# Order of the copies of turned weights, of the odd head's sign and of the value products in the slots of a top-k attention with a routed expert layer

## The chip, the cores and the metric

The kernel runs on one core of one Trainium2 chip. The metric is the device time of one execution in microseconds (us). A time "before" is given as the median of three runs; the profile is that of one further execution.

## What is computed

The reference makes attention over the 32 largest scores of each row, and puts every resulting token through the one expert that its gate chooses. Cut to what matters:

```python
B, H, S, D = 8, 8, 576, 64
scores = q @ k.T / sqrt(D)                      # per batch and head
kth    = the 32nd largest score of each row
attn   = exp(scores - max), zero where scores < kth, divided by its row sum
x      = (attn @ v) as [B*S, H*D]               # 4608 tokens of 512
e      = argmax(x @ w_gate)                     # one of 8 experts per token
out    = softmax weight * sigmoid(x @ w_output_gate)[e] * (relu(x @ w1[e]) @ w2[e])
```

## The kernel before, in words

Queries are taken 128 at a time: 36 tiles of queries (`NTT`), and in each tile four pairs of heads (`NHP`). One pair of heads of one tile is a **step**; there are 144 (`NSTEP`), and the main loop (L939) runs over them with four more to drain. Each pass of the loop is a slot in which the work of several steps stands, each at another stage. Nothing reorders it: every engine runs its instructions in the order in which the loop issues them. For step i:

- `scores` (L282), called two slots ahead: TensorE makes the scores of both heads in PSUM (L293), and ScalarE copies them to SBUF (L301).
- `gmax` and `rank` (L305, L322): VectorE finds the largest scores of eight groups of columns, and from those the first 24 of each row.
- `below` (L346): ScalarE marks, for each of the two heads, the scores below the 24th (a Sign, L355), and GpSimd adds the marks to the scores (L358). `window` (L372) is VectorE's search for the next eight in that, and `choose` (L380) takes the 32nd score out of them.
- `exps` (L366): ScalarE takes the exponential (L370).
- In slot i+1 the scores under the 32nd are cleared: `weigh` (L396) does it on VectorE (L404). In the first 36 steps (i under `LONE`, which is 36) the odd head of the pair goes another way, and I call these the **lone steps**: `veil` (L408) makes a Sign on ScalarE (L411) and a sum on GpSimd (L414), and `unveil` (L417) takes the exponential of that sum on ScalarE (L420) at the slot's end. There is no exponential of that head in `exps` then.
- In slot i+2 `flip` (L423) turns the weights on TensorE, 128x128 at a time, in three parts of four, one and four pieces (L430), and ScalarE copies each part out of PSUM (L438). I call them first, second and third flip. Their PSUM tiles `pst` come from a pool of two buffers in turn: the third flip writes into the buffer of the first, so it waits for the first flip's copy. The second flip's one piece holds the last 64 columns of the even head and the first 64 of the odd one, so in a lone step it waits for `unveil`.
- In slot i+4, for even i, `attend` (L443) multiplies two steps' weights with the values (L462, "the products with values"), and ScalarE copies the result (L464).

Some slots carry **side work** in the PSUM tile of the second flip: for each tile of queries `gates` (L489) and `rows` (L500) in two slots that follow each other, and one product for each group of tiles (L565). ScalarE copies their results behind the second flip's (L486, L496).

The expert layer's work stands in the same slots, from about step 37 on, one piece of a tile of 128 tokens in each slot (`heavy_piece`, L855): L757 for the first matrix, L772 for the second, and L746 for the turning of the tokens (`turn`, L742), which also takes a `pst` buffer. What remains of it runs after the last step.

In a slot, before the change, TensorE has: first flip, expert piece, second flip with side work, third flip, turning of tokens, scores of step i+2, and for even i the products with values. ScalarE has: the two signs of `below`, the odd head's sign (`veil`), the copy of the last products, the copy of the first flip, the exponentials, the expert piece's result, the copies of the second flip and of side work, that of the third, the turned tokens, the copy of the scores, `unveil`.

Of the kernel before, what the change touches and what calls it, by code (L numbers as in the profile page):

```python
# [31 lines left out]
SUMS = 1.3  # L32
# [7 lines left out]
def tile_topk_attention_moe(  # L40
# [11 lines left out]
    nc = tc.nc  # L52
    NTT, D, H, _ = qa.shape
    NB, _, _, S = ka.shape
# [58 lines left out]
    ident = consts.tile([P, P], F32, name="ident")  # L113
# [81 lines left out]
    def run(exact, stack):  # L195
# [22 lines left out]
        spent = [0.0]  # L218
# [7 lines left out]
        def run_slow(budget, kinds):  # L226

            for x in [x for x in slow if x[2] in kinds]:
                if spent[0] + x[3] > budget:
                    return  # L230
                slow.remove(x)
                spent[0] += x[3]
                x[4]()
# [88 lines left out]
        def rank(i, r):  # L322
            if exact:
                return
            vs, cs = VV[i]
            part = [c.rearrange("p (g j) -> p g j", j=8)[:, :, :(2, 5, 8)[r]] for c in cs]
            for a in range(2):
                nc.vector.max(out=vs[:, a, 8 * r:8 * r + 8], in_=part[a])  # L328
            if r < 2:
                for a in range(2):  # L330
                    nc.vector.match_replace(out=part[a], in_to_replace=vs[:, a, 8 * r:8 * r + 8],  # L331
                                            in_values=part[a], imm_value=LOW)
# [3 lines left out]
        def lone(i, a):  # L336
            return a == 1 and not exact and i < LONE
# [70 lines left out]
        def veil(i):  # L408

            if lone(i, 1):  # L410
                nc.scalar.activation(marks[2].bitcast(I8).rearrange("p (s b) -> p s b", b=2)[:, :, 1], SC[i, 1], AF.Sign,  # L411
                                     bias=LESS.pop(i))
                w = wk.tile([P, S], F32, name="w", bufs=3)
                nc.gpsimd.tensor_tensor(w, SC.pop((i, 1)), marks[2], op=ALU.add)  # L414
                VE[i] = w
# [4 lines left out]
                nc.scalar.activation(EP[i][:, 1, :], VE.pop(i), AF.Exp, bias=VV.pop(i)[0][:, 1, 32:33], scale=SCALE,  # L420
                                     accum_out=SM[t][:, 2 * hp + 1:2 * hp + 2])

        def flip(i, part, extra=None):  # L423

            pt = EP[i].rearrange("p a s -> p (a s)")
            c0, c1 = ((0, 4), (4, 5), (5, 9))[part]
            n = c1 - c0
            ps = ps_t.tile([P, 4, P], F32, name="pst")
            for c in range(c0, c1):
                nc.tensor.transpose(ps[:, c - c0, :], pt[:, c * P:(c + 1) * P], ident)  # L430
            ev = extra(ps) if extra else None
            x = wk.tile([P, n, P], F32, name=f"pT{n}", bufs=6 if n == 4 else 3)
            PTT.setdefault(i, []).append(x)
            if part == 2:
                del EP[i]

            def copies():
                nc.scalar.activation(x, ps[:, :n, :], AF.Copy)  # L438
                if ev:
                    ev()  # L440
            return copies

        def attend(i):  # L443

            t, hp = divmod(i, NHP)
            if hp == 0:
                XT[t] = st.tile([P, NC, P], F32, name="xT", bufs=2)
            pT = [PTT.pop(i + k) for k in range(2)]
            po = ps_o.tile([P, 2, P], F32, name="po")
            for half in (True, False):  # L450
                for k in range(2):
                    for m, (b, _) in enumerate(TT[t]):
                        qs = slice(0, P) if len(TT[t]) == 1 else slice(m * 64, (m + 1) * 64)
                        for c in (4,) if half else range(4):
                            for a in range(2):
                                if half:
                                    lhs = V[b][:, 32 + 2 * (hp + k) + a, :]
                                    rhs = pT[k][1][:, 0, qs]
                                else:
                                    lhs = V[b][:, (2 * (hp + k) + a) * 4 + c, :]  # L460
                                    rhs = pT[k][2 * a][:, c, qs]
                                nc.tensor.matmul(po[a * 64:(a + 1) * 64, k, qs], lhs, rhs, start=half and not k and not m,  # L462
                                                 stop=(c == 3 and k == 1 and m == len(TT[t]) - 1))
            return lambda: nc.scalar.activation(XT[t][:, hp:hp + 2, :], po, AF.Copy)  # L464
# [329 lines left out]
        NSTEP = NTT * NHP  # L794

        LONE = 4 * ENDS[0] + 12 if ENDS else 0
# [34 lines left out]
        def fetch_ahead():  # L831

            for what, f in (("w1", fetch_w1), ("w2", fetch_w2)):
                ahead(what, f, 1 if heavy else 2)

        def ahead_of_slot():

            clock[0] += 1
            fetch_ahead()
# [21 lines left out]
        def side_start():  # L861

            f = side.popleft() if side else None

            def start(ps):
                copies, use = f(ps)
                uses.append(use)
                return copies
            return f and start
# [65 lines left out]
            gmax(0, a)  # L935

        attended = []

        for i in range(NSTEP + 4):  # L939
            t, hp = divmod(i, NHP)  # L940
            step[0] = i
            for r in range(3):
                if i < NSTEP:
                    rank(i, r)
                    if r == 0:
                        shift(i)
                fill(1)
            if 1 <= i <= NSTEP:
                choose(i - 1)
                fill(2)  # L950
                weigh(i - 1)
            if i < NSTEP:
                below(i)
            if 1 <= i <= NSTEP:
                veil(i - 1)
            spent[0] = 0.0
            run_slow(SUMS, ("x",))
            spent[0] = 0.0
            while attended:
                attended.pop()()  # L960
            early, late = [], []
            if 2 <= i < NSTEP + 2:
                early.append(flip(i - 2, 0))
            ahead_of_slot()
            heavy_start()
            ev = heavy_piece()
            if ev:
                late.append(ev)
            if 2 <= i < NSTEP + 2:
                late.append(flip(i - 2, 1, side_start()))  # L970
            if i >= NSTEP + 2:
                extra = side_start()
                if extra:
                    late.append(extra(ps_t.tile([P, 4, P], F32, name="pst")))
            room = not uses
            if 2 <= i < NSTEP + 2:
                late.append(flip(i - 2, 2))
            ev = turn_ahead() if room else None
            if ev:
                late.append(ev)  # L980
            if i + 2 < NSTEP:
                late.append(scores(i + 2))
            if 4 <= i < NSTEP + 4 and i % 2 == 0:
                attended.append(attend(i - 4))
            for f in early:
                f()
            if i < NSTEP:
                exps(i)
            for f in late:
                f()  # L990
            if 1 <= i <= NSTEP:
                unveil(i - 1)
            if i + 1 < NSTEP:
                gmax(i + 1, 0)
                gmax(i + 1, 1)
            if i < NSTEP:
                window(i, 0)
                window(i, 1)
            ahead("x", fetch_x, 2, "id", 1)
            run_slow(DMAS if i < LONE else MORE, ("table", "ids", "out"))  # L1000
            side_use()
            fill(3)
            if i < NSTEP:
                if hp == 0 and t + 2 < NTT:
                    load_q(t + 2)
                if i == 0:
                    small.extend(([] if exact else setup()) + [clear_ids])
                jj = t % 9
                b2 = t // 9 * 2
                for j0, b in ((0, b2 + 1), (5, b2 + 2)):  # L1010
                    n = (jj - j0) * NHP + hp
                    if b < NB:
                        if n == 1:
                            load_k(b)
                        if n == 6:
                            load_v(b)
            if i >= 3 and (i - 3) % NHP == NHP - 1:
                tt = (i - 3) // NHP
                if tt == GROUPS[gi][0]:
                    LGT[gi] = st.tile([P, max(map(len, GROUPS)), 16], F32, name="lg", bufs=2)  # L1020
                tile_rows(tt, gi, LGT[gi], tt - GROUPS[gi][0])
                if tt == GROUPS[gi][-1]:
                    gi += 1
# [117 lines left out]
    with ExitStack() as stack:  # L1141
        run(False, stack)
# [47 lines left out]
```

## Time and profile before

| what | value |
|---|---|
| median of 3 runs | 1285.65 us (1284.1 to 1286.22) |
| the profiled execution's own time | 1284.37 us |
| its span, first to last instruction | 1282.5 us |
| mean granted TensorE clock | 0.955 |
| TensorE busy | 1166.4 us (91%) |
| VectorE busy | 1072.1 us (84%) |
| ScalarE busy | 966.7 us (75%) |
| GpSimd busy | 711.7 us (55%) |

The busy times of the whole span mix three stages: the lone steps up to about 272 us, the steps with expert work up to about 1078 us, and the rest of the expert work. In rows of the profile PE is TensorE, PEld its loading of weights, DVE VectorE, ACT ScalarE, POOL GpSimd and SP the queue that issues most DMAs; L430 is line 430 of the kernel. PEclk is the share of TensorE's full clock that was granted.

### The profile page before, as it was taken

How to read it: one execution, taken by the hardware profiler on the slowest of the kernel's cores; microseconds unless marked ns; L12 is line 12 of the kernel's file. 1: busy time of each engine (PE TensorE's matmuls, PEld its weight loads, DVE VectorE, ACT ScalarE, POOL GpSimd, SP SyncE). 2: the span in 40 equal slices, each digit the busy share in tenths (PEclk: the TensorE clock that was granted, in tenths of full speed). 3: DMA queues.
4: the chain of work that ended last, by engine and by line, in shares of the span. 5: the costliest groups of instructions: out<-in, count | busy, mean ns of one | idle time of the engine just before them, and what ended most of it. 6: DMA issues, size and time to landing. Idle time of an engine off the chain costs nothing.

```text
span 1282.5 us, 30773 instructions
## 1 busy us (share of the span) xinstructions
PE 1166.4 (91%) x9771; PEld 890.8 (69%) x9771; DVE 1072.1 (84%) x6097; ACT 966.7 (75%) x1896; POOL 711.7 (55%) x1120
## 2 busy tenths in 40 slices
PE   5676677779999899999999999999999999999996
PEld 3454455457777677777777777777777777799995
DVE  6888889999999989999999999999999996264442
ACT  5788889888888778888887888888788886353542
POOL 5565656775547744596745775545865584312110
PEclk7788888889999899999999999999999999999998
DMA  5400021723654676456265665576464445799980
GB/s 136 77 17 18 18 54 55 279 58 89 225 177 139 182 256 218 168 184 219 107 220 165 200 222 196 170 262 213 157 201 165 156 156 200 264 396 361 364 327 21
DMA packets 113733, 227.45 MB, mean 177 GB/s; under 512 B 19206, under 2 KB 37894, under 8 KB 112528
## 3 DMA queue, kind: packets, MB, share of 16 engines
q1 hardware_dynamic: 104176, 205.67, 48.1%
q0 software_dynamic: 7552, 18.96, 4.3%
q8 instruction: 81, 1.33, 0.4%
q10 hardware_dynamic: 1824, 0.67, 0.3%
q14 instruction: 100, 0.82, 0.2%
HBM read 206.68 MB, written 20.69 MB: 177 GB/s over the span
## 4 chain that ended last, share of the span: by engine, by line
PE 54%; issue 14%; DVE 12%; ACT 9%; POOL 9%; DMA 1%; POOLq 0%; ACTq 0%; DVEq 0%
PE pm L757 13%; PE pm L772 12%; PE ps L293 9%; PE po L462 9%; PE pst L430 8%; POOL w L358 5%; ACT marks L355 4%; DVE cand L331 2%; DVE v L328 2%; DVE v L375 2%; ACT ep L370 2%; DVE cand L320 2%; ACT ep L420 1%; PE pst L746 1%; PE pst L483 1%
## 5 line engine op out<-in xcount | busy, mean ns | idle before, releaser
L358 POOL TENSOR_TENSOR w<-s,marks 128x576 f32<-128x576 f32 x288 | 363.1, 1282 | 315.4 <-ACT marks L355 201.6
L320 DVE MAX8 cand<-s 128x8 f32<-128x72 f32 x2304 | 323.9, 218 | 29.5 <-ACT s L301 29.0
L430 PE MATMUL pst<-ident,ep 128*128 128x128 f32 x1296 | 219.5, 288 | 86.5 <-ACT pT L438 56.3
L757 PE MATMUL pm<-xs,w1t 128*128 128x128 f32 x2560 | 297.1, 275 | 0.8 <-ACT xs L749 0.8
L757 PEld LDWEIGHTS pm<-xs,w1t 128*128 128x128 f32 x2560 | 292.0, 192 | 2.1 <-ACT xs L749 1.1
L430 PEld LDWEIGHTS pst<-ident,ep 128*128 128x128 f32 x1296 | 149.8, 144 | 163.3 <-ACT pT L438 83.5
L375 DVE MAX8 v<-w 128x8 f32<-128x576 f32 x288 | 211.4, 750 | 53.6 <-POOL w L358 44.9
L438 ACT ACTIVATE pT<-pst 128x512 f32<-128x512 f32 (+1 forms) x432 | 206.0, 488 | 43.9 <-PE pst L430 33.8
L355 ACT ACTIVATE marks<-s,v 128x576 int8<-128x576 f32 x288 | 219.9, 767 | 12.3 <-DVE v L328 7.4
L301 ACT ACTIVATE s<-ps 128x1152 f32<-128x1152 f32 (+1 forms) x145 | 163.0, 1125 | 79.8 <-PE ps L293 79.1
L293 PE MATMUL ps<-kst,qst 64*128 64x288 f32 (+1 forms) x1280 | 197.3, 463 | 5.1 <-ACT s L301 5.1
L772 PE MATMUL pm<-w2t,ht 128*128 128x512 f32 x448 | 201.4, 593 | 0.0
L404 DVE SCALAR_TENSOR_TENSOR ep<-s,kth,ep 128x576 f32<-128x576 f32 x252 | 197.4, 815 | 0.3 <-ACT xu L486 0.3
L462 PEld LDWEIGHTS po<-pT,v 128*64 128x64 f32 x3200 | 171.9, 146 | 34.9 <-issue 34.9
L462 PE MATMUL po<-pT,v 128*64 128x128 f32 (+1 forms) x3200 | 188.4, 278 | 0.0
L370 ACT ACTIVATE ep<-s,v 128x576 f32<-128x576 f32 x252 | 182.5, 767 | 2.6 <-POOL v L344 2.5
L293 PEld LDWEIGHTS ps<-kst,qst 64*128 64x128 f32 (+1 forms) x1280 | 104.6, 190 | 50.9 <-issue 26.1
L772 PEld LDWEIGHTS pm<-w2t,ht 128*128 128x128 f32 x448 | 80.8, 190 | 80.8 <-issue 80.8
L783 POOL DMA_INDIRECT out_dram<-y,idt x40 | 47.4, 1185 | 145.9 <-ACT y L779 121.7
L328 DVE MAX8 v<-cand 128x8 f32<-128x16 f32 (+2 forms) x864 | 127.9, 188 | 0.0
L331 DVE MATCH_REPLACE8 cand<-v,cand 128x16 f32<-128x16 f32 (+1 forms) x576 | 95.0, 173 | 0.0
L1060 DVE TENSOR_TENSOR w2l<-w2t,w2h 128x2048 fp32r<-128x2048 f32 x24 | 54.3, 2290 | 25.0 <-ACT w2h L1059 25.0
(167 smaller groups left out, 1206.6 us busy)
## 6 DMA issues: line engine op xcount, KB each, us to landing
w1t<-in_w_dram SPq DMA_DIRECT2D x40, 2048.0 KB, 9.4
w2t<-in_w_dram SPq DMA_DIRECT2D x40, 2048.0 KB, 11.8
x_rows<-xu SPq DMA_DIRECT2D x36, 256.0 KB, 2.1
qst<-in_qa_dram SPq DMA_DIRECT2D x70, 128.0 KB, 11.2
v<-in_va_dram SPq DMA_DIRECT2D x8, 1024.0 KB, 6.0
kst<-in_ka_dram SPq DMA_DIRECT2D x14, 576.0 KB, 7.8
v<-in_va_dram SPq DMA_DIRECT2D x16, 64.0 KB, 5.5
ids<-far SPq DMA_DIRECT2D x1, 678.0 KB, 9.8
```

The costliest lines, as they stand in the source:

```text
L293: nc.tensor.matmul(ps[qs, a, n, :288], Q[t][rows, hp, qs], K[b][rows, hp, cols], start=True, stop=True)
L320: nc.vector.max(out=c[:, 8 * g:8 * g + 8], in_=SC[i, a][:, g * GW:(g + 1) * GW])
L355: nc.scalar.activation(m.bitcast(I8).rearrange("p (s b) -> p s b", b=2)[:, :, 1], s, AF.Sign, bias=vs[:, a, PIVOT - 1:PIVOT], scale=-(1.0 ...
L358: x = nc.gpsimd.tensor_tensor(w, s, m, op=ALU.add)
L370: nc.scalar.activation(EP[i][:, a, :], SC[i, a], AF.Exp, bias=VV[i][0][:, a, 32:33], scale=SCALE)
L375: nc.vector.max(out=VV[i][0][:, a, 24:32], in_=SW[i][0][a])
L404: LAST[0] = nc.vector.scalar_tensor_tensor(e, SC.pop((i, a)), kth_col(i, a), e, op0=ALU.is_ge, op1=ALU.mult, accum_out=SM[t][:, 2 * hp + a ...
L430: nc.tensor.transpose(ps[:, c - c0, :], pt[:, c * P:(c + 1) * P], ident)
L438: nc.scalar.activation(x, ps[:, :n, :], AF.Copy)
L462: nc.tensor.matmul(po[a * 64:(a + 1) * 64, k, qs], lhs, rhs, start=half and not k and not m, stop=(c == 3 and k == 1 and m == len(TT[t]) - 1))
L757: nc.tensor.matmul(ph[:, f - f0, :], w[:, c, f * P:(f + 1) * P], XS[s][:, c, :], start=(c == 0), stop=(c == NC - 1))
L772: nc.tensor.matmul(PY[s], HT[s][:, f, :], w[:, f, :], start=(f == 0), stop=(f == NF - 1))
```

## The change

The order of the loop's slot is altered in four places. First, `veil` (and the scaling of finished tokens on GpSimd, `run_slow` with "x") is issued behind the functions in `early` and no longer ahead of them; the copy of the last products is therefore issued ahead of it. Second, the second flip stands right behind the first, its copy in `early` too, in all lone steps and in every other slot that has no side work; a later slot with side work keeps the old place. Third, in lone steps with even i the products with values stand between second and third flip, and their copy stands in the same slot, behind the exponential; from step 36 on they stay at the slot's end. Fourth, in lone steps with odd i and no side work, twelve turns of the identity (`IDLE`) are added behind the second flip, into a part of its PSUM tile that nothing reads. In the program that runs this happens in eight slots, 3, 5, 9, 13, 17, 21, 25 and 33, which makes 96 added matmuls.

```diff
-        def flip(i, part, extra=None):
+        def flip(i, part, extra=None, idle=0):
...
             ev = extra(ps) if extra else None
+            for _ in range(idle):
+                nc.tensor.transpose(ps[:, 3, :], ident, ident)
...
+        IDLE = 12
...
             if i < NSTEP:
                 below(i)
-            if 1 <= i <= NSTEP:
-                veil(i - 1)
-            spent[0] = 0.0
-            run_slow(SUMS, ("x",))
-            spent[0] = 0.0
             while attended:
                 attended.pop()()
             early, late = [], []
+            extra = side_start() if i < NSTEP + 2 else None
             if 2 <= i < NSTEP + 2:
                 early.append(flip(i - 2, 0))
+                if i < LONE or not extra:
+                    early.append(flip(i - 2, 1, extra, idle=0 if i >= LONE or extra or i % 2 == 0 else IDLE))
+            if 4 <= i < LONE and i % 2 == 0:
+                late.append(attend(i - 4))
             ahead_of_slot()
             heavy_start()
             ev = heavy_piece()
             if ev:
                 late.append(ev)
-            if 2 <= i < NSTEP + 2:
-                late.append(flip(i - 2, 1, side_start()))
+            if 2 <= i < NSTEP + 2 and i >= LONE and extra:
+                late.append(flip(i - 2, 1, extra))
...
-            if 4 <= i < NSTEP + 4 and i % 2 == 0:
+            if max(4, LONE) <= i < NSTEP + 4 and i % 2 == 0:
                 attended.append(attend(i - 4))
             for f in early:
                 f()
+            if 1 <= i <= NSTEP:
+                veil(i - 1)
+            spent[0] = 0.0
+            run_slow(SUMS, ("x",))
+            spent[0] = 0.0
             if i < NSTEP:
                 exps(i)
             for f in late:
```

Lines behind L430 move down by two or more in the new file: L438 becomes L440, L462 becomes L464.

On ScalarE, slot 5, a lone step without side work, before: two signs, the odd head's sign, the copies with the exponential among them, the scores, `unveil`.

```order
L355 ACTIVATE marks_80,n<-s,v_591 128x576
L355 ACTIVATE marks_81,n<-s,v_591 128x576
L411 ACTIVATE marks_82<-s,less 128x576
L464 ACTIVATE xT<-po 128x256
L438 ACTIVATE pT_652<-pst 128x512
L370 ACTIVATE ep<-s,v_591 128x576
L438 ACTIVATE pT_655<-pst 128x128
L438 ACTIVATE pT_661<-pst 128x512
L301 ACTIVATE s<-ps 128x1152
L420 ACTIVATE ep,sums<-w,v_487 128x576
```

The same slot now:

```order
L355 ACTIVATE marks_80,n<-s,v_604 128x576
L355 ACTIVATE marks_81,n<-s,v_604 128x576
L440 ACTIVATE pT_661<-pst 128x512
L440 ACTIVATE pT_676<-pst 128x128
L411 ACTIVATE marks_82<-s,less 128x576
L370 ACTIVATE ep<-s,v_604 128x576
L440 ACTIVATE pT_682<-pst 128x512
L301 ACTIVATE s<-ps 128x1152
L420 ACTIVATE ep,sums<-w,v_499 128x576
```

The copies of first and second flip (128x512 and 128x128) stand ahead of the odd head's sign, and the copy of the products (xT) has gone to the slot before.

On TensorE, slots 2 to 4, before: flips of 9 pieces, scores of four matmuls, and from slot 4 the products with values (po) behind the scores.

```order
L430 MATMUL pst<-ident,ep 128x128 x9
L293 MATMUL ps<-kst,qst 128x288 x4
L430 MATMUL pst<-ident,ep 128x128 x9
L293 MATMUL ps<-kst,qst 128x288 x4
L430 MATMUL pst<-ident,ep 128x128 x9
L293 MATMUL ps<-kst,qst 128x288 x4
L462 MATMUL po<-pT_382,v_120 64x128 x2
```

Slots 2 to 4 now, up to the first products:

```order
L430 MATMUL pst<-ident,ep 128x128 x9
L293 MATMUL ps<-kst,qst 128x288 x4
L430 MATMUL pst<-ident,ep 128x128 x5
L433 MATMUL pst<-ident 128x128 x12
L430 MATMUL pst<-ident,ep 128x128 x4
L293 MATMUL ps<-kst,qst 128x288 x4
L430 MATMUL pst<-ident,ep 128x128 x5
L464 MATMUL po<-pT_379,v_120 64x128 x2
```

The twelve turns of the identity (L433) stand between second and third flip of slot 3, and the products between second and third flip of slot 4.

On ScalarE, a slot with expert work, no side work and a turning of tokens (xs), before:

```order
L438 ACTIVATE pT_4377<-pst 128x512
L370 ACTIVATE ep<-s,v_4321 128x576 x2
L765 ACTIVATE ht<-pm 128x512
L438 ACTIVATE pT_4402<-pst 128x128
L438 ACTIVATE pT_4408<-pst 128x512
L749 ACTIVATE xs<-pst 128x512
L301 ACTIVATE s<-ps 128x1152
```

The same slot now:

```order
L440 ACTIVATE pT_4473<-pst 128x512
L440 ACTIVATE pT_4476<-pst 128x128
L370 ACTIVATE ep<-s,v_4417 128x576 x2
L767 ACTIVATE ht<-pm 128x512
L440 ACTIVATE pT_4504<-pst 128x512
L751 ACTIVATE xs<-pst 128x512
L301 ACTIVATE s<-ps 128x1152
```

The copy of the second flip has moved ahead of the two exponentials and of the expert piece's result. VectorE's order is unchanged; on GpSimd and in SP's queue only the scaling of finished tokens and its store come one slot earlier in lone steps.

## The prediction

> **What bounds the kernel now.** I read the page first, for the stages.
>
> ```profile
> span 1282.5 us, 30773 instructions
> PE   5676677779999899999999999999999999999996
> PEclk7788888889999899999999999999999999999998
> ```
>
> TensorE is only 60 to 70% busy in the first slices, at a clock of 0.7 to 0.8, and full from the tenth slice on. So the two stages have different limits, and I took them apart by a table of windows, one for lone steps and one for steps with expert work; the rows of the odd head's sign give the pace of the first.
>
> ```profile
> 60.00:240.00 180.00, 128.29 (x1156) 90.98 (x1156) 161.70 (x1015) 155.75 (x335) 108.76 (x138) 0.85 0.18 55
> 300.00:1080.00 780.00, 769.95 (x6717) 575.05 (x6715) 728.51 (x4350) 638.93 (x1290) 486.52 (x798) 1.00 0.56 188
> L411 ACT ACTIVATE marks<-s,less x36: 761/765/769, 18.8 to 273.5; 128x576 int8<-128x576 f32 x36
> ```
>
> Columns are PE, PEld, DVE, ACT, POOL, clock, DMA share, GB/s. Lone steps: 36 signs from 18.8 to 273.5 are 35 steps in 254.7 us, 7.28 us each, and no engine is full: VectorE works 161.70/180 x 7.28 = 6.54 us of a step, ScalarE 6.30. Steps with expert work: TensorE is 98.7% busy, so there only what TensorE waits for counts.
>
> The timeline of one lone slot (the start of step 16, which has side work) shows the chain that makes 7.28 out of 6.54. Columns: start, duration, engine, line; in brackets the idle time before and who ended it.
>
> ```profile
> 120.58 0.77 ACT L355 ACTIVATE marks<-s,v 128x576 int8<-128x576 f32 x1
> ...
> 127.42 0.77 ACT L355 ACTIVATE marks<-s,v 128x576 int8<-128x576 f32 x1
> 127.57 0.33 PE L430 MATMUL pst<-ident,ep 128*128 128x128 f32 x1 [1.42 <-ACT ep L420]
> 128.18 0.77 ACT L355 ACTIVATE marks<-s,v 128x576 int8<-128x576 f32 x1
> 128.94 0.77 ACT L411 ACTIVATE marks<-s,less 128x576 int8<-128x576 f32 x1
> 129.60 0.58 ACT L438 ACTIVATE pT<-pst 128x512 f32<-128x512 f32 x1
> 130.08 0.77 ACT L370 ACTIVATE ep<-s,v 128x576 f32<-128x576 f32 x1
> 130.23 1.12 PE L430 MATMUL pst<-ident,ep 128*128 128x128 f32 x4 [2.01 <-ACT pT L438]
> 130.74 0.26 ACT L438 ACTIVATE pT<-pst 128x128 f32<-128x128 f32 x1
> 130.89 1.28 POOL L414 TENSOR_TENSOR w<-s,marks 128x576 f32<-128x576 f32 x1
> 131.28 2.20 PE L293 MATMUL ps<-kst,qst 64*64 64x288 f32 x16
> 133.54 1.13 ACT L301 ACTIVATE s<-ps 128x1152 f32<-128x1152 f32 x1 [1.56 <-PE ps L293]
> 134.57 0.77 ACT L420 ACTIVATE ep<-w,v 128x576 f32<-128x576 f32 x1
> 135.33 0.77 ACT L355 ACTIVATE marks<-s,v 128x576 int8<-128x576 f32 x1
> ```
>
> Two signs, the odd head's sign and the first flip's copy run in a row on ScalarE; only then may TensorE make the third flip (it idled 2.01 us) and the scores, for which ScalarE in turn idles 1.56 us; the scores' copy, `unveil` and the next signs follow. This slot takes 135.33 - 127.42 = 7.91 us; the one before takes 127.42 - 120.58 = 6.84.
>
> The difference is the clock: third flip and scores run at half speed here. The same work at full clock, and the products with values fast and slow:
>
> ```profile
> 136.64 0.76 PE L430 MATMUL pst<-ident,ep 128*128 128x128 f32 x5
> 138.41 0.66 PE L430 MATMUL pst<-ident,ep 128*128 128x128 f32 x4 [1.01 <-ACT pT L438]
> 139.00 1.20 PE L293 MATMUL ps<-kst,qst 64*64 64x288 f32 x16
> 609.92 2.40 PE L462 MATMUL po<-pT,v 128*64 128x128 f32 x40
> 118.66 3.84 PE L462 MATMUL po<-pT,v 128*64 128x128 f32 x40
> ```
>
> So scores cost 1.20 or 2.20, a third flip 0.66 or 1.12, products 2.40 or up to 3.84; one more turn in a row costs 0.76 - 0.66 = 0.1 us. What the clock follows is seen in stretches of 3.41 us, laid where it changes:
>
> ```profile
> 125.05:128.47 3.42, 1.76 (x20) 0.84 (x9) 3.38 (x28) 3.27 (x7) 0.66 (x4) 1.00 0.02 5
> 128.47:131.88 3.41, 1.65 (x12) 1.09 (x16) 2.83 (x12) 3.30 (x8) 3.41 (x3) 0.50 0.00 0
> ...
> 135.29:138.71 3.42, 2.41 (x34) 2.00 (x31) 2.50 (x14) 3.42 (x10) 2.38 (x2) 1.00 0.00 0
> 138.71:142.12 3.41, 2.08 (x24) 1.05 (x22) 3.21 (x21) 2.85 (x7) 2.83 (x6) 1.00 0.01 4
> 142.12:145.53 3.41, 0.99 (x7) 0.64 (x7) 3.05 (x19) 3.41 (x9) 2.48 (x3) 1.00 0.49 150
> 145.53:148.95 3.42, 3.42 (x20) 2.39 (x22) 3.32 (x23) 1.83 (x4) 1.60 (x4) 0.50 0.02 7
> 148.95:152.36 3.41, 2.98 (x45) 2.28 (x41) 2.79 (x19) 3.41 (x9) 1.83 (x2) 1.00 0.02 5
> ```
>
> After a stretch with TensorE busy 1.76 or 0.99 us the clock is 0.50; after 2.41 or 2.08 it stays 1.00, and after one full stretch at 0.50 it is 1.00 again. The mean of 0.85 over 180 us is 0.15/0.5 x 180 = 54 us at half clock, 16 such stretches in 24.7 steps, or 22 in the 34 lone steps from 2 to 35.
>
> **The change part by part.** *The sign moves behind the copies.* GpSimd adds the odd head's marks at 130.89, after its two other sums, though the sign was over at 128.94 + 0.77 = 129.71: 1.18 us of delay hide there, and 0.64 (the two copies, 0.48 and 0.16 from start to start) is what it gets, more where the second flip is late (side work, 0.3 to 0.5). Were that cover gone, `unveil`, 134.57 - 130.89 - 1.28 = 2.4 us behind that sum, has room for the rest. So the move is free, and the first flip's copy, the third flip and the scores come 129.60 - 128.94 = 0.66 us earlier.
>
> *A lone slot at full clock, without side work.* Starts on ScalarE in the rows above are 0.76 apart for a sign, 0.66 for the odd head's sign and the exponential, 0.48 and 0.16 for the copies, 1.03 for scores, 0.76 for `unveil`. Odd slot: 0.76 + 0.76 + 0.48 + 0.16 + 0.66 + 0.66 + 0.48 + 1.03 + 0.76 = 5.75 us. TensorE is not later: the twelve turns start at about 0.26 and end at 0.26 + 12 x 0.1 = 1.5, plus the 0.2 by which one turn alone (0.33) is longer; the second flip's copy waits for the last of them (one tile), but ScalarE gets there only at 2.0. The third flip starts at 2.1, when the first's copy is done, and the scores end at about 3.9, as ScalarE comes for them (3.96). Even slot: second flip at 0.15, products to 0.26 + 2.40 = 2.66, third flip's four pieces to 3.1, scores to 4.35, their copy and `unveil` 1.79: 6.2 us. Side work adds one or two copies like the second flip's (0.26), an estimate of 0.2 to 0.5. Each is under VectorE's 6.54, whose order does not change, so VectorE is late next. It has little slack to catch up with, so I take 6.6: (7.28 - 6.6) x 34 = 23.1 us less.
>
> *The clock.* The 1.42 us of idle in front of the second flip stays: it waits for `unveil`, whatever the order. In odd slots without side work the turns leave only 1.5 to 2.1 idle behind it, and in even slots the products leave nothing. But the slots with `gates` get neither: second flip and gates end near 1.0 and the third flip waits until 2.1, so 1.42 + 1.1 = 2.5 us of idle can fall into one stretch, more than the 1.66 after which the clock fell at 125.05. These are 8 slots; I take 10 stretches at half clock in all where there were 22. A slot with one costs 7.91 - 6.84 = 1.07 us by the rows above, from nothing (it falls where VectorE is late anyway) to 1.7 (half of 3.41). 10 x 1.07 gives back 10.7 us. Sum of the lone steps: -12.4.
>
> *Steps with expert work.* TensorE waits there in one place only that the change touches.
>
> ```profile
> L746 PE MATMUL pst<-ident,xg 128*128 128x128 f32 x100 | 16.9, 292 | 6.7 <-ACT pT L438 6.7
> ...
> 592.13 0.67 ACT L779 ACTIVATE y<-pm,idt 128x512 f32<-128x512 f32 x1
> 592.70 0.76 ACT L438 ACTIVATE pT<-pst 128x128 f32<-128x128 f32 x2
> 593.02 0.66 PE L746 MATMUL pst<-ident,xg 128*128 128x128 f32 x4 [0.82 <-ACT pT L438]
> ```
>
> The first row is of 300 to 1080 us. The turning of tokens takes the second flip's buffer and waits for its copy, which stood behind two exponentials and the expert result. With that copy right behind the first flip's it is long done. All 6.7 us go, TensorE being full; nothing that I see takes their place, since first and second flip need weights and buffers of the slot before. Bounds: 0 and, with the starts that hide under the modelled ends, 8.
>
> **Sum.** -12.4 - 6.7 = -19.1 against the profiled execution's 1284.37 (span 1282.5 and 1.87 around it): 1265.3. That execution is 1.28 under the median of the three; from the median it would be 1266.6. I say 1266. About 0.2%, 2.6 us, is what a measurement of this kernel can tell from no change.
>
> **Rivals.** *No half clock is left, VectorE sets the pace* (chance 0.17). For: where TensorE is fed in each stretch the clock never falls. Against: the slots with `gates`. (7.28 - 6.54) x 34 = 25.2, and 6.7: 1253. The Trainium skill ("TensorE: Matmul & The Clock Gate", Architectural detail and the section on oscillation) has the clock fall only after more than about 3.4 us without work, and by that rule there would be none; the stretches above disagree, since it fell after one with 1.76 us of work.
>
> *The clock stays as it is* (0.15): the idle in front of the second flip is enough, with 22 stretches. 23.1 - 22 x 1.07 = -0.4 saved in the lone steps, 6.7 in the others: 1278.
>
> *Turns do not keep the clock up* (0.05). Then the eight slots with twelve turns fall as well, 18 stretches: 23.1 - 19.3 + 6.7 = 10.5 saved, 1274. Against it stands the program's start, where TensorE makes 24 turns of the identity and nothing else; their first and their last (count, then shortest, median and longest in ns):
>
> ```profile
> L897 PE MATMUL po<-ident x8: 421/421/475, 1.4 to 2.9; 128*128 128x128 f32 x8
> L897 PE MATMUL po<-ident x5: 272/273/334, 5.5 to 6.0; 128*128 128x128 f32 x5
> ```
>
> A turn falls from 421 ns to 273 within the group, so the clock rose on turns alone. The Trainium skill ("TensorE: Matmul & The Clock Gate", Part 4: PE-mode transpose) says that turns do not count as work for the clock; this row contradicts it.
>
> *The products at half clock are now in the path, and it ends slower* (0.09). Before, products stood behind the scores, beside scores' copy and `unveil`; now they stand ahead of third flip and scores, and a stretch at half clock there costs the full 1.7 us. For it: 3.84 against 2.40. Against: a slot with products has TensorE busy in a row, and the row from 145.53 shows that one full stretch brings the clock back. It decides from (23.1 + 6.7)/1.7 = 18 stretches on; at 24, 40.8 - 29.8 = 11 us slower: 1295.
>
> **How the numbers follow.** The forecast, 8 to 12 stretches at half clock and most of the 6.7 us, has 0.54: 1266. The range reaches to the first rival (1251) and just over the second (1279), and leaves out the last and some tails. Faster by over 0.2%: forecast, first and third rival, and nearly all of the second, 0.88. Within: 0.05, from the second's upper end and a mild form of the last. Slower: 0.07.
>
> **What would show it.** Right: signs of the odd head under 6.9 us apart on average; mean clock from 60 to 240 us about 0.92; the wait of the turned tokens for the second flip's copy gone; in lone slots no idle of ScalarE for the scores of over 1 us. Wrong: a clock of 0.85 or less there; TensorE's products of over 3 us in most even slots; ScalarE waiting for the last turn of the identity; the steps with expert work no shorter, or a new wait of TensorE in them.

## The result and the profile after

| | before | changed |
|---|---|---|
| median of 4 runs, same chip | 1285.62 us | 1255.3 us (1253.79 to 1256.3) |
| span of the profiled execution | 1282.5 us | 1252.4 us |
| mean granted TensorE clock | 0.955 | 0.97 |
| 35 lone steps, odd head's sign first to last | 254.7 us | 237.2 us |
| rest of the span | 1027.8 us | 1015.2 us |

The ratio is 0.9765 (95% interval 0.9748 to 0.9782): 30.3 us faster, inside the range, where 19 us were forecast. The span lost 30.1 us, 17.5 of them in the lone steps and 12.6 in the rest. From the page before, the flips on TensorE and the scores' copy on ScalarE, two of the groups with much idle time ahead of them (the figure behind the second bar, with what ended most of it):

```profile
L430 PE MATMUL pst<-ident,ep 128*128 128x128 f32 x1296 | 219.5, 288 | 86.5 <-ACT pT L438 56.3
...
L301 ACT ACTIVATE s<-ps 128x1152 f32<-128x1152 f32 (+1 forms) x145 | 163.0, 1125 | 79.8 <-PE ps L293 79.1
```

The page of the changed kernel, with its clock and the same two groups:

```profile
span 1252.4 us, 30982 instructions
...
PEclk7989997889999999999999999999999999999998
...
L430 PE MATMUL pst<-ident,ep 128*128 128x128 f32 x1296 | 222.1, 288 | 75.2 <-ACT ep L420 52.3
...
L301 ACT ACTIVATE s<-ps 128x1152 f32<-128x1152 f32 (+1 forms) x145 | 163.2, 1126 | 53.4 <-PE ps L293 48.0
```

TensorE's waits ahead of the flips were for copies before (56.3 us); now most are for the odd head's exponential (L420, 52.3). ScalarE's wait for the scores fell from 79.8 to 53.4 us. The rows that answer to those of the two stages, the pace of the odd head's sign and the turned tokens (the last row is of 270 to 1050 us, all expert steps):

```profile
60.00:240.00 180.00, 132.42 (x1246) 94.87 (x1242) 168.22 (x1068) 163.83 (x351) 120.70 (x157) 0.90 0.25 82
300.00:1050.00 750.00, 746.19 (x6583) 562.27 (x6582) 709.91 (x4251) 617.23 (x1256) 475.96 (x785) 1.00 0.58 194
L411 ACT ACTIVATE marks<-s,less x36: 762/778/827, 19.3 to 256.5; 128x576 int8<-128x576 f32 x36
L748 PE MATMUL pst<-ident,xg 128*128 128x128 f32 x104 | 15.6, 273 | 0.0
```

A lone step takes 237.2/35 = 6.78 us where it took 7.28. The mean clock from 60 to 240 us is 0.90 where it was 0.85. The turned tokens wait for nothing.

Two lone slots of the changed kernel, steps 16 and 17, show what is left. Timeline, columns as before:

```profile
117.95 0.81 ACT L355 ACTIVATE marks<-s,v 128x576 int8<-128x576 f32 x1
118.15 0.33 PE L430 MATMUL pst<-ident,ep 128*128 128x128 f32 x1 [1.82 <-ACT ep L420]
118.73 4.07 PE L464 MATMUL po<-pT,v 128*64 128x128 f32 x40
122.85 0.38 ACT L466 ACTIVATE xT<-po 128x256 f32<-128x256 f32 x1 [0.99 <-PE po L464]
123.32 1.20 PE L293 MATMUL ps<-kst,qst 64*64 64x288 f32 x16
124.59 1.13 ACT L301 ACTIVATE s<-ps 128x1152 f32<-128x1152 f32 x1 [0.56 <-PE ps L293]
126.37 0.77 ACT L355 ACTIVATE marks<-s,v 128x576 int8<-128x576 f32 x1
126.69 1.47 PE L433 MATMUL pst<-ident 128*128 128x128 f32 x12
128.52 0.66 PE L430 MATMUL pst<-ident,ep 128*128 128x128 f32 x4 [0.36 <-ACT pT L440]
129.11 1.20 PE L293 MATMUL ps<-kst,qst 64*64 64x288 f32 x16
130.38 1.13 ACT L301 ACTIVATE s<-ps 128x1152 f32<-128x1152 f32 x1
132.16 0.77 ACT L355 ACTIVATE marks<-s,v 128x576 int8<-128x576 f32 x1
```

The even slot takes 8.42 us: its products run 4.07 us, mostly at half clock, and stand on the way to the scores. The odd slot takes 5.79, and ScalarE waits for nothing in it. At full clock the products take 2.40 us, and an even slot with side work like this one takes 6.75 (experiment 7).

### The profile page after: what moved, and what is told of

The parts are those of the page before. It is cut to its first block, busy times and chain, and to the rows that moved or that the text cites. A ratio compares the mean times of both kernels' runs of the same rounds, so it can differ in the third digit from the quotient of the medians.

```text
span 1252.4 us, 30982 instructions
## 1 busy us (share of the span) xinstructions
PE 1157.2 (92%) x9867; PEld 891.3 (71%) x9867; DVE 1066.4 (85%) x6097; ACT 959.7 (77%) x1896; POOL 711.0 (57%) x1120
## 4 chain that ended last, share of the span: by engine, by line
PE 65%; DVE 13%; issue 12%; POOL 6%; ACT 2%; DMA 1%; POOLq 0%; ACTq 0%; DVEq 0%
PE pm L759 15%; PE pm L774 15%; PE po L464 11%; PE ps L293 10%; PE pst L430 10%; DVE cand L320 4%; POOL w L358 3%; DVE v L375 3%; DVE cand L331 2%; DVE v L328 2%; DVE ep L404 2%; PE pst L485 1%; PE pst L748 1%; DMA w2t<-in_w_dram 1%; ACT marks L355 1%
## 5 line engine op out<-in xcount | busy, mean ns | idle before, releaser
L430 PE MATMUL pst<-ident,ep 128*128 128x128 f32 x1296 | 222.1, 288 | 75.2 <-ACT ep L420 52.3
L430 PEld LDWEIGHTS pst<-ident,ep 128*128 128x128 f32 x1296 | 149.2, 144 | 162.4 <-ACT ep L420 61.2
L440 ACT ACTIVATE pT<-pst 128x512 f32<-128x512 f32 (+1 forms) x432 | 201.6, 487 | 39.0 <-PE pst L430 30.5
L301 ACT ACTIVATE s<-ps 128x1152 f32<-128x1152 f32 (+1 forms) x145 | 163.2, 1126 | 53.4 <-PE ps L293 48.0
L293 PE MATMUL ps<-kst,qst 64*128 64x288 f32 (+1 forms) x1280 | 186.1, 440 | 5.1 <-ACT s L301 5.1
L464 PEld LDWEIGHTS po<-pT,v 128*64 128x64 f32 x3200 | 166.9, 142 | 25.5 <-issue 24.4
L464 PE MATMUL po<-pT,v 128*64 128x128 f32 (+1 forms) x3200 | 184.0, 273 | 0.2 <-issue 0.2
L293 PEld LDWEIGHTS ps<-kst,qst 64*128 64x128 f32 (+1 forms) x1280 | 100.1, 181 | 48.1 <-issue 24.2
```

What stands on the lines that cost most here:

```text
L293: nc.tensor.matmul(ps[qs, a, n, :288], Q[t][rows, hp, qs], K[b][rows, hp, cols], start=True, stop=True)
```

## The experiments

In the tables "lone" is the stretch of 35 steps by the odd head's sign; the expectations count steps 2 to 35 only, which gives 247.5 us before and 229.5 for the changed kernel. "Rest" is the span without the lone stretch. Each lone figure is of one profiled execution; where the lone steps of two kernels are the same program, the figures agree within 0.4 us (254.7 and 254.8, 238.6 and 238.7, 237.2 and 236.8). Ratios are to the kernel before, run beside it on the same chip.

**1. The expert steps' part alone.**

```diff
...
+            extra = side_start() if i < NSTEP + 2 else None
...
+                if i >= LONE and not extra:
+                    early.append(flip(i - 2, 1))
...
-            if 2 <= i < NSTEP + 2:
-                late.append(flip(i - 2, 1, side_start()))
+            if 2 <= i < NSTEP + 2 and (i < LONE or extra):
+                late.append(flip(i - 2, 1, extra))
```

> The kernel before with one part of the change: from step 36 on, in slots without side work, the second flip and its copy stand right behind the first; the lone steps are as before. Theory (TensorE is the limit there, and the turned tokens waited longer than the trace's idle column says): all of the 12.3 us by which the expert steps got shorter, so 1273 us against 1285.6, and the starts of the scores in slots with a turning of tokens as in the changed kernel. Rival (only the idle that the trace shows, 6.7 us, belongs to this part, the rest came from the lone steps' earlier end): 1279. Rival (the two stages are tied by transfers): the lone steps change too.

Measured 1272.14 us, ratio 0.9887 (0.9861 to 0.9913). Lone 254.8, rest 1015.1, as in the changed kernel: this edit alone makes the whole of the second stage's gain, and does nothing to the first. Why 12.3 (the whole 30.3 less the 18.0 of steps 2 to 35) and not 6.7 is seen from the start of one slot's scores to the next's. Before, a slot with a turning of tokens:

```profile
586.39 1.24 PE L293 MATMUL ps<-kst,qst 64*128 64x288 f32 x8
...
591.49 0.71 PE L430 MATMUL pst<-ident,ep 128*128 128x128 f32 x5
593.02 0.66 PE L746 MATMUL pst<-ident,xg 128*128 128x128 f32 x4 [0.82 <-ACT pT L438]
593.61 1.24 PE L293 MATMUL ps<-kst,qst 64*128 64x288 f32 x8
```

The same slot in the changed kernel:

```profile
562.38 1.24 PE L293 MATMUL ps<-kst,qst 64*128 64x288 f32 x8
...
567.59 0.60 PE L430 MATMUL pst<-ident,ep 128*128 128x128 f32 x4
568.03 0.60 PE L748 MATMUL pst<-ident,xg 128*128 128x128 f32 x4
568.56 1.24 PE L293 MATMUL ps<-kst,qst 64*128 64x288 f32 x8
```

593.61 - 586.39 = 7.22 against 568.56 - 562.38 = 6.18: 1.04 us less where the idle column said 0.82. The turned tokens now start 0.44 us after the third flip, and each group's shown end reaches past the next one's start; an idle time counts only from that shown end. Taken so over all slots with a turning of tokens, five lost 1.04 to 1.05 us, four 0.72 to 0.82, one 1.62, one 0.48, and sixteen 0.15 each, in which the column showed no idle at all: 12.8 together, of which 0.5 comes back elsewhere.

**2. The sign behind the first flip's copy, alone.**

```diff
-            if 1 <= i <= NSTEP:
-                veil(i - 1)
-            spent[0] = 0.0
-            run_slow(SUMS, ("x",))
-            spent[0] = 0.0
...
             for f in early:
                 f()
+            if 1 <= i <= NSTEP:
+                veil(i - 1)
+            spent[0] = 0.0
+            run_slow(SUMS, ("x",))
+            spent[0] = 0.0
```

> The kernel before with one part: the odd head's sign and the scaling of finished tokens stand behind the first flip's copy; second flip, products and turns as before. Theory (the copy came 0.66 us earlier, and this counts in slots in which ScalarE waits for the scores, that is mostly the even ones): about 17 slots x 0.66 = 11 us less, 1274, with the clock from 60 to 240 us at 0.85 as before. Rival (the clock alone made the gain in the lone steps): within 4 us of before. Rival (the sign's delay is felt by GpSimd and VectorE): slower than before.

Measured 1268.24 us, ratio 0.9858 (0.9832 to 0.9883): more than the 11 us expected. Lone 238.6 us, against 237.2 with the whole change. Its window from 60 to 240 us:

```profile
60.00:240.00 180.00, 132.20 (x1184) 91.59 (x1184) 170.64 (x1077) 163.95 (x354) 121.27 (x155) 0.86 0.24 79
```

And the timeline of step 16, the one shown of before:

```profile
118.84 0.81 ACT L355 ACTIVATE marks<-s,v 128x576 int8<-128x576 f32 x1
120.36 0.63 ACT L438 ACTIVATE pT<-pst 128x512 f32<-128x512 f32 x1
121.04 1.11 PE L430 MATMUL pst<-ident,ep 128*128 128x128 f32 x4 [1.34 <-ACT pT L438]
122.08 2.19 PE L293 MATMUL ps<-kst,qst 64*64 64x288 f32 x16
124.35 1.13 ACT L301 ACTIVATE s<-ps 128x1152 f32<-128x1152 f32 x1 [1.11 <-PE ps L293]
126.14 0.77 ACT L355 ACTIVATE marks<-s,v 128x576 int8<-128x576 f32 x1
```

The clock is 0.86 where it was 0.85; third flip and scores are at half speed. The slot takes 126.14 - 118.84 = 7.30 where the same slot before took 7.91: the copy comes 1.52 us behind the first sign (2.18 before), and everything behind it moves up by that. Odd slots gain too (6.42 and 6.08 where 6.82 and 6.74 stood), which I had not expected: there as well ScalarE had waited for the scores. The gain is uneven: over steps 2 to 35 it is 0.49 us a slot on average. Slots 6 and 14, which half clock no longer touches, gain 2.2 and 2.1 us, and five slots lose up to 0.3. So 16 of the 17.5 us in the lone steps come from this edit, at a clock that is nearly the same. It also moves the scaling of finished tokens on GpSimd and the place of the products' copy on ScalarE; these I did not run apart from the sign.

**3 to 5. Turns, and the products' place.** Without the turns:

```diff
-        IDLE = 12
+        IDLE = 0
```

> The changed kernel without the twelve turns of the identity in eight slots. Theory (they keep the clock up): more stretches at half clock, 18 instead of 12 in the lone steps, 6 x 1.5 = 9 us more than the changed kernel, about 1264, clock from 60 to 240 us near 0.85. Rival (turns do not count for the clock, or the order alone made the gain): 1255, the clock as with them.

Products back at the slot's end (number 4), and that without turns (number 5):

```diff
-            if 4 <= i < LONE and i % 2 == 0:
-                late.append(attend(i - 4))
...
-            if max(4, LONE) <= i < NSTEP + 4 and i % 2 == 0:
+            if 4 <= i < NSTEP + 4 and i % 2 == 0:
```

> The changed kernel with the products with values back at the slot's end in lone steps; early second flip and the turns stay. Theory (products between the flips keep the clock up in even slots and cost nothing at full clock): even slots have TensorE idle for 2 us ahead of the third flip again and fall to half clock, about 20 stretches, lone steps near 236 us, 6 us slower than the changed kernel: 1261. Rival (products in the middle only lengthen the way to the scores, by up to 8.8 us slots when the clock is low): lone steps near 225, 1250.

> The changed kernel without turns and with the products back at the slot's end: what is left is the sign behind the copies and the early second flip, in lone steps and in slots with expert work. Theory (the sign's move alone made the lone steps' gain, and the products in the middle without turns lost 11 us of it): lone steps near 231 us as with the sign alone, expert steps near 787, 1256, as the changed kernel. Rival (the early second flip is what costs in the run without turns): lone steps near 241, 1266.

| lone steps have | us | ratio | lone, us | clock 60 to 240 us |
|---|---|---|---|---|
| sign's move only (2) | 1268.24 | 0.9858 (0.9832 to 0.9883) | 238.6 | 0.86 |
| and early second flip (5) | 1258.03 | 0.9791 (0.9763 to 0.9819) | 242.0 | 0.81 |
| and turns, products last (4) | 1262.23 | 0.982 (0.9794 to 0.9846) | 245.6 | 0.83 |
| and products in the middle, no turns (3) | 1266.35 | 0.9845 (0.9818 to 0.9872) | 249.4 | 0.82 |
| all (changed kernel) | 1255.3 | 0.9765 (0.9748 to 0.9782) | 237.2 | 0.90 |

(Number 2 lacks the expert steps' part, so its total is not to be compared with the others; the lone column is.) The theory on the turns held: without them the lone steps take 12.2 us more (9 were expected), and the clock is 0.82. Number 4 came out near the 1261 us expected. That the products in the middle lose without turns held too, at 7.4 us and not 11. For the early second flip in lone steps the rival was right in part: it is no gain, 3.4 us are lost against the sign's move alone. Turns without the products' move lose 3.6 more, the products' move without turns 7.4 more. Where the 3.6 go is in the waits of ScalarE from 30 to 250 us in number 4 (total, times, longest):

```profile
ACT pT L440 <- PE pst L433: 4.9, 7, 1.1
```

The second flip's copy waits there for the last of the twelve turns; the changed kernel's view has no such row. Only together, turns and the products' move bring the lone steps back to where the sign's move alone had them.

**6. That claim by itself: the sign's move and the expert steps' part, nothing else.** The edits of 1 and 2 together, with the changed kernel run again beside it.

> The kernel before with two edits alone: the sign behind the first flip's copy, and in slots with expert work and no side work the second flip right behind the first. Theory (these two make nearly all of the change's gain; early second flip in lone steps, products in the middle and turns together net 1 to 2 us): lone steps 231, expert steps 787, 1256 to 1258, and the changed kernel in the same call 1255. Rival (the parts work on each other and the sum does not hold): over 1262.

> The changed kernel again, to stand beside the two others on the same chip: 1255 within 3 us by every theory; its lone steps 229 to 230 us if the stretches at half clock fall the same way in each execution, some us apart if they depend on where the stretches happen to lie.

Measured 1253.33 us, ratio 0.9763 (0.9745 to 0.978); the changed kernel beside it 1252.77, 0.9761 (0.9744 to 0.9778). Both came out 2 to 4 us under what was expected, and the same: two edits make the whole gain, and their parts add up (lone 238.7 us, rest 1013.4).

**7. More turns, ahead of the second flip.** They stand where TensorE waits 1.42 us for the odd head's exponential, ten in each lone slot, in the changed kernel.

```diff
...
+            for _ in range(ahead):
+                nc.tensor.transpose(ps[:, 3, :], ident, ident)
             for c in range(c0, c1):
...
-                    early.append(flip(i - 2, 1, extra, idle=0 if i >= LONE or extra or i % 2 == 0 else IDLE))
+                    early.append(flip(i - 2, 1, extra, idle=0 if i >= LONE or extra or i % 2 == 0 else IDLE,
+                                      ahead=10 if i < LONE else 0))
```

> The changed kernel with ten more turns of the identity ahead of the second flip's piece in each lone slot, where TensorE waits 1.42 us for the odd head's exponential. Theory (what the lone steps still lose is half clock, and VectorE's floor is less than the 6.54 us that I took from its busy time): no half clock from 30 to 250 us, every slot between 5.8 and 6.7, 6.3 on average, 15 us less than the changed kernel: 1240. Rival (VectorE's 6.54 holds): 34 x 6.54 = 222 against 229.6, 1248. Rival (ten turns are longer than the gap and delay the second flip): slower than the changed kernel, over 1257.

Measured 1244.37 us, ratio 0.967 (0.9645 to 0.9695): faster than the changed kernel by 11 us, 4 short of the theory. Lone 227.7 us; the clock and 16 steps (8 to 23) from sign to sign, with the same 16 steps of the kernel before in the fence behind:

```profile
60.00:240.00 180.00, 156.25 (x1594) 120.03 (x1594) 175.16 (x1121) 171.04 (x368) 128.28 (x168) 0.99 0.25 82
63.29:164.42 101.13, 90.54 (x959) 69.39 (x960) 100.25 (x642) 98.25 (x214) 69.86 (x88) 0.98 0.13 34
```

```profile
70.03:185.89 115.86, 81.25 (x756) 57.02 (x756) 102.36 (x643) 99.60 (x215) 69.90 (x88) 0.84 0.12 30
```

VectorE works 100.25 of 101.13 us: with the clock up it is the limit, as the prediction said, but at 6.27 us a step and not 6.54. For the same 16 steps of before its busy time is 102.36/16 = 6.40: my window from 60 to 240 us held later steps as well, and the busy time itself shrank by 2% as the steps came closer together. Over all lone steps 6.5 us a step are reached, since the later ones are longer.

Three variants of it: products at the slot's end; the ten turns without the twelve; six turns in place of ten.

> Ten turns ahead of the second flip in each lone slot and the twelve behind it in odd ones, but the products back at the slot's end. Theory (at full clock the place of the products does not matter, since VectorE is full at 6.27 us a step): 1244 within 3 us. Rival (products in the middle are needed to feed TensorE ahead of the third flip): half clock in even slots again, over 1250. Rival (products in the middle stand in the way of the scores): under 1241.

> Ten turns ahead of the second flip in each lone slot, without the twelve behind it in odd slots; products between second and third flip. Theory (the clock fell where the idle ahead of the second flip and another idle fell into one stretch, so filling the one that is in every slot is enough): 1244 within 3 us, clock from 60 to 240 us over 0.97. Rival (the idle ahead of the third flip in odd slots is enough for half clock by itself): 1250 or more.

> The changed kernel with six turns ahead of the second flip in each lone slot, where ten gave 1244. They fill 0.6 to 0.7 of the 1.42 us. Theory (the clock falls after a stretch of 3.41 us with over 1.4 to 1.6 us of idle, and with 0.8 left only the slots with side work on gates reach that, 0.8 + 0.9): a few stretches, 3 to 6, 1246 to 1250. Rival (any idle left ahead of the second flip is enough): 12 stretches as in the changed kernel, 1255. Rival (ten were too many): under 1243.

| turns ahead / behind second flip, products | us | ratio | lone, us | clock |
|---|---|---|---|---|
| 10 / 12, in the middle | 1244.37 | 0.967 (0.9645 to 0.9695) | 227.7 | 0.99 |
| 6 / 12, in the middle | 1245.61 | 0.9704 (0.9687 to 0.972) | 231.1 | 0.95 |
| 10 / 0, in the middle | 1250.31 | 0.9722 (0.9693 to 0.975) | 233.2 | 0.93 |
| 10 / 12, at the end | 1262.14 | 0.9809 (0.9778 to 0.9839) | 246.5 | 0.95 |

Six turns came out 0.4 us under the 1246 to 1250 us expected. Without the twelve, the idle ahead of the third flip was enough for half clock in places, so filling one gap is not enough (from 172.73 to 176.14 us TensorE worked 1.44 us and idled 1.67 ahead of a third flip, and the next stretch was at 0.50): that theory fell, by 6 us. And the products at the end are 18 us slower though the clock is 0.95: the theory that their place does not matter at full clock fell as well. An odd slot of that kernel, at full clock and with side work, shows a part of why:

```profile
88.14 2.40 PE L466 MATMUL po<-pT,v 128*64 128x128 f32 x40
90.04 0.77 ACT L355 ACTIVATE marks<-s,v 128x576 int8<-128x576 f32 x1
90.97 1.25 PE L430 MATMUL pst<-ident 128*128 128x128 f32 x10
92.06 0.27 PE L432 MATMUL pst<-ident,ep 128*128 128x128 f32 x1
93.09 0.28 ACT L442 ACTIVATE pT<-pst 128x128 f32<-128x128 f32 x1 [0.68 <-PE pst L487]
93.68 0.79 ACT L411 ACTIVATE marks<-s,less 128x576 int8<-128x576 f32 x1
94.61 1.28 POOL L414 TENSOR_TENSOR w<-s,marks 128x576 f32<-128x576 f32 x1 [0.68 <-ACT marks L411]
```

The products run into the odd slot and push the flips behind them; the second flip's copy now stands ahead of the odd head's sign on ScalarE and makes it wait 0.68 us, the sign starts 3.64 us into the slot, and GpSimd, too, waits for it. The cover that made the sign's delay free is used up there. In odd slots without side work the twelve turns do the same. ScalarE's waits for the second flip's tile from 30 to 250 us, behind the turns (L435) and behind side work (L487):

```profile
ACT pT L442 <- PE pst L435: 8.1, 7, 1.9
ACT pT L442 <- PE pst L487: 5.6, 7, 1.3
```

That is 13.7 us, where the kernel with the products in the middle has neither wait; its lone steps are 18.8 us shorter. So the products' place and the turns act together. How much of the 18.8 us would be left without the twelve turns is open, since that I did not run. The same kind of wait may be why the early second flip alone (number 5) loses 3.4 us: ScalarE's copies wait there 3.2 us for flips and side work, against 0.4 in number 2. But the clock is lower too, 0.81 against 0.86, and I did not take the two apart.

## Why the prediction was right, point by point

- *What bounds the lone steps* held: the way over the first flip's copy, third flip and scores. The sign's move is worth 0.49 us a slot on average, and not its 0.66 in each. An odd slot with turns, at full clock, took 5.79 us where 5.75 were worked out.
- *The sum of the lone steps* gave 12.4 us and 18.0 were measured on the same steps, but the terms were wrong in kind. I let full clock bring each step to 6.6 us (23.1 less) and took 10 stretches at half clock off at 1.07 us. By these terms nothing is saved if the clock stays (the second rival: -0.4), though the copy coming 0.66 us earlier stood in the same text; it entered the sum only as part of the way to 6.6. Measured, the sign's move alone brings 16.6 on these steps with the clock at 0.86 for 0.85, and second flip, products and turns net 1.4 us. "The clock" as the source of the gain is the step that failed.
- *The range:* that 1255.3 lies within it is in part luck. The range reached down to 1251 for the rival in which no half clock is left, at 1253; the time came near that one, but with the clock at 0.90.
- *Half clock:* the mean clock came to 0.90, 0.92 was forecast. Over steps 2 to 35 it is 0.90 as well, which makes 46 us or 13 to 14 stretches where 10 were forecast (before: 0.82, 26 stretches and not 22). A stretch that falls on the products costs the 1.7 of the slower rival and not 1.07: the even slot above took 8.42 us, the same slot at full clock 6.75.
- *VectorE as what is late next* held in experiment 7, at 6.27 us for 6.54.
- *One sign of being right failed:* ScalarE still waited for the scores in lone slots, 19 times from 60 to 250 us, 10.6 us in all and 1.4 at the longest, where no wait of over 1 us was to be left.
- *Expert steps:* the mechanism was right, the size was not: 12.3 for 6.7, over the bound of 8, mainly since the idle column leaves out what lies under the shown ends. A smaller part is the window: from 275 us on, the column shows 8.1 us, since two turnings at 284 and 291 us stand ahead of the 300 us from which I read it.
- *The slower rival* was the right mechanism at a smaller size: products at half clock in the path make the lone steps slower than with the sign's move alone (number 3, by 10.8 us, of which the early second flip has 3.4 and the products 7.4), and the twelve turns pay for it.
- *Turns and the clock:* with ten turns in each lone slot and twelve more in eight of them the clock is 0.99; the changed kernel without any has 0.82. The rule of the Trainium skill ("TensorE: Matmul & The Clock Gate", Part 4: PE-mode transpose) that turns do not count is contradicted by that too, for the turns of this kernel, which the profile records as MATMUL without telling their mode.

## What to carry to other kernels

Where an engine runs in order, look for the instruction whose result nobody needs soon that stands ahead of one for which two engines wait; moving it was worth 0.49 us a round here, of the 0.66 by which it stood in the way, at nearly the same clock. When several edits go in together, run each alone: here two small moves made the whole gain, and three that belong together paid only for each other. The idle column of TensorE was too low a price here (0.82 us shown, 1.04 gained); take it from the start of one round's fixed work to the next's.

## What the runs showed of the hardware

Filling TensorE's waits with turns of the identity raised the granted clock from 0.90 to 0.99 and gave 11 us more (1244.37 against 1255.3), although they are no work for the result. The clock fell after stretches in which TensorE was about half busy, not only after empty ones; in the changed kernel:

```profile
115.80:119.20 3.40, 1.58 (x16) 1.17 (x18) 3.37 (x27) 3.40 (x8) 1.33 (x4) 1.00 0.00 0
119.20:122.60 3.40, 3.40 (x36) 3.27 (x32) 3.37 (x17) 2.66 (x7) 3.40 (x3) 0.50 0.00 0
122.60:126.00 3.40, 2.51 (x28) 1.35 (x24) 3.06 (x24) 2.39 (x4) 1.60 (x5) 1.00 0.24 86
```

1.58 of 3.40 us busy, and the next stretch is at 0.50; it is full, and the one after is at 1.00 again. No sharp limit comes out of these runs: before, the clock stayed at 1.00 after a stretch with 2.08 us of work, and in the kernel with ten turns of experiment 7 it fell after one with 2.16:

```profile
157.62:161.03 3.41, 2.16 (x21) 1.25 (x21) 3.38 (x22) 3.41 (x11) 2.13 (x2) 1.00 0.00 0
161.03:164.44 3.41, 3.41 (x17) 2.52 (x14) 3.37 (x22) 3.19 (x7) 1.97 (x4) 0.50 0.00 0
```
